# Warm-up operand made before the masks, first k issued by ScalarE, dilated q and k in 72 rows, and a new table of durations

## Chip, cores and metric

The kernel runs on one core of a Trainium2 chip. The metric is the device time of one execution in microseconds (us). Runs of the kernel before: 850.34 us median of 3 (850.1 to 851.13).

## What is computed

Attention with 8 heads over 4 batches of 576 tokens, head size 64, then two pairs of dense layers on the 2304 resulting rows of 512 features. Heads 0 to 3 see a window of the last 32 tokens (plain), heads 4 to 7 every fourth of the last 128 tokens (dilated). All is float32.

```python
mask_plain = (rel >= 0) & (rel < window)                                  # window = 32
mask_dil = (rel >= 0) & (rel < window * dilation) & (rel % dilation == 0) # dilation = 4
scores = np.where(masks[None, :, :, :], scores, -1000000000.0)
attn = np.exp(scores - np.max(scores, axis=-1, keepdims=True))
attn = attn / (np.sum(attn, axis=-1, keepdims=True) + 1e-09)
x = np.matmul(attn, v)            # -> (2304, 512)
h = x @ w_in;  x = (h - np.tanh(h)) @ w_out                               # first layer pair, d_ff 2048
h = x @ w_in2; out = (h * (1.0 / (1.0 + np.exp(-h)))) @ w_out2            # second layer pair
```

## The kernel before

A matrix product in the dense layers is made of three passes in a shorter float type (`passes`): each operand is split into a leading part and the rest. The weights of the first layer pair therefore go through a chain before TensorE may use them (class `Chunk`): a load on SP's queue (`load`), two steps on ScalarE (`prelu`, L203, and `lows`, L208), one on VectorE (`shift`, L213), one on GpSimd (`join`, L217), the leading part on ScalarE (`leading`, L169) and the rest on VectorE or GpSimd (`trailing`, L226).

The tokens are cut into five blocks, the first of 512 columns. While the first block goes through the first layer pair (16 slices f of d_ff, each with 12 matmuls `h<-x,w` and 12 `y<-gg,w`), the attention of the second batch is computed beside it. Ahead of that stands the attention of the first batch: four pairs of heads, c = 0 and 1 plain, c = 2 and 3 dilated. For each pair q, k and v are loaded; TensorE transposes q and k (`transpose_pe`) into a PSUM bank, half a tensor at a time; ScalarE or VectorE moves the half into qT or kT (`transposed`, through the helper at L169 to L173); then come scores (`products`, L458 and L467), maxima, exponentials (L516 or L525), sums, `normed` (L537), a transposition (L560), the product with v (`halves`, L576) and the split of the result into X (`x_hi` on ScalarE at L169, `x_lo` on VectorE at L631).

The pairs' q and k come in as rows of consecutive tokens (`load_in`): a plain pair as 96 rows of six tokens, a dilated pair as 128 rows of four tokens and a second piece of 16 rows. A plain tensor takes 2 loads (one for each head) and 6 transpositions of 96 rows; a dilated tensor 4 loads and 8 transpositions (128 and 16 rows for each of four classes).

The order of this whole stretch, up to the end of the first block, is set by a planner that runs when the program is built (`play`): every step is an `Op` with the engines that can take it and a cost on each, a rank, and for loads a landing time; the planner places the steps one by one on in-order engines. So a change of its costs moves steps on every engine. Where it expects TensorE to wait it puts in small matmuls on the constant `one` (`idle`, L109). Loads that SP and ScalarE issue share eight completion semaphores in turn; an issue waits for the load that had its semaphore before.

Ahead of the planned part stands a prologue in program order: the constants, `build_near()` (masks on GpSimd with three copies on VectorE, L270 to L278), then `warm`, set on VectorE (L1055), twelve matmuls on it (L1059), and one exponential on ScalarE over `warm` itself (L1060), which loads ScalarE's table.

```python
        build_near()
        warm = cpool.tile([P, 512], BF16, name="warm")
        nc.vector.memset(warm, 1.0)
        ...
        for n in range(WARM):
            nc.tensor.matmul(bank, warm[:, 0:P], warm, start=True, stop=True)
        nc.scalar.activation(out=warm[:, 0:1], in_=warm[:, 0:1], func=AF.Exp)
```

Of the kernel before, what the change touches and what calls it, by code (L numbers as in the profile page):

```python
# [8 lines left out]
F32 = mybir.dt.float32  # L9
# [10 lines left out]
P = 128  # L20
QB = 64
ROWS_P = 96
# [13 lines left out]
def tile_kernel(  # L36
# [251 lines left out]
    class Pair:  # L288
# [20 lines left out]
        def load_in(self, which, src):  # L309
            b, h0 = self.b, 2 * self.c  # L310
            if self.first:
                if self.dil:
                    t = wpool.tile([P, 2, DIL, 2, D], F32, tag="win", name=which)
                    parts = [(t[:, 0], src[b, h0:h0 + 2, :DIL * P]), (t[:CLS - P, 1], src[b, h0:h0 + 2, DIL * P:])]
                else:
                    t = wpool.tile([ROWS_P, S // ROWS_P, 2, D], F32, tag="win", name=which)
                    parts = [(t, src[b, h0:h0 + 2])]
                return t, [lambda e, j=j, out=out, x=x: e.dma_start(out=out[:, :, j], in_=x[j].rearrange("(p i) d -> p i d", i=out.shape[1]))  # L318
                           for out, x in parts for j in range(2)]
# [94 lines left out]
        def transpose_pe(self, which, half):  # L414

            dst = (self.qT, self.kT)[which]
            src = (self.qin, self.kin)[which]
            bank = ps_h.tile([P, 512], F32, tag="h", name="h")
            n = S // 2
            if self.dil:  # L420
                rest = CLS - P
                for m in range(2):
                    r, a = 2 * half + m, CLS * m
                    nc.tensor.transpose(bank[:, a:a + P], src[:, 0, r].rearrange("p j d -> p (j d)"), one[F32])
                    nc.tensor.transpose(bank[:, a + P:a + CLS], src[:rest, 1, r].rearrange("p j d -> p (j d)"), one[F32][:rest, :rest])
                self.moved = dst[:, n * half:n * (half + 1)], bank[:, :n]
            else:
                k = S // ROWS_P // 2
                for m in range(k):
                    i = k * half + m  # L430
                    nc.tensor.transpose(bank[:, ROWS_P * m:ROWS_P * (m + 1)], src[:, i].rearrange("p j d -> p (j d)"), one[F32][:ROWS_P, :ROWS_P])
                self.moved = (dst.rearrange("p (r i) -> p i r", i=2 * k)[:, k * half:k * (half + 1)],
                              bank[:, :n].rearrange("p (i r) -> p i r", i=k))
            return self.moved
# [554 lines left out]
    LANES, LAG_P, LAG_V = 8, 3.0, 2.0  # L989
# [35 lines left out]
    with tc.manual_schedule():  # L1025
# [27 lines left out]
        build_near()  # L1053
# [6 lines left out]
        nc.scalar.activation(out=warm[:, 0:1], in_=warm[:, 0:1], func=AF.Exp)  # L1060
# [8 lines left out]
        turned.append(opool.tile([P, NV, 2, 2, 32], F32, tag="wout", name="turned"))  # L1069
        in_room, out_room, stages = {}, {}, [(st1, NF * 2)]  # L1070
        for p in first:
            for w in range(2):
                got[p, w] = [op(QK_ON[p.c], fn, rank=p.c + 0.1 * w, late=0.6 if not p.dil or n < 2 else 0.1) for n, fn in enumerate(p.pieces(w))]
# [18 lines left out]
        for i, (p, (n0, n1)) in enumerate(units):  # L1092
            g, m = (n0, n1), n1 - n0
            r = p.rank + UNIT * n0 / NB
            if n0 == 0:
                moves = []
                for which in range(2):
                    for half in range(2):
# [3 lines left out]
                        moves.append(op({"V": 0.5, "A": 0.58} if p.dil else {"V": 0.38, "A": 0.31}, lambda e, p=p, w=which, held=held: p.transposed(e, w, held["m"]),  # L1102
# [28 lines left out]
            for z in range(2):  # L1131
                b = op({"A": 0.22 if p.dil else 0.33}, lambda e, p=p, n0=n0, z=z: p.x_hi(e, (n0, z)), [a], r)
                ends.append(op({"V": 0.23 if p.dil else 0.31}, lambda e, p=p, n0=n0, z=z: p.x_lo((n0, z)), [b], r))
# [19 lines left out]
        for n, ch in enumerate(chunks(0, w_in1, w_out1)):  # L1153
# [7 lines left out]
            b = op({"A": 0.57}, lambda e, ch=ch: ch.prelu(e), [a], due)  # L1161
            c = op({"A": 0.58}, lambda e, ch=ch: ch.lows(e), [a], due, port=True)
# [3 lines left out]
            b = op({"A": 0.56}, lambda e, ch=ch: ch.leading(e), [c, last_lead[ch.is_in], *room.get(f, ())], due, port=True)  # L1166
            last_lead[ch.is_in] = b
            c = op({"V": 0.75, "P": 1.3}, lambda e, ch=ch: ch.trailing(e), [b], due, port=True)
# [19 lines left out]
        def front(p):  # L1188
# [5 lines left out]
            a = op({"V": 1.09}, lambda e, p=p: p.transpose(0), [q_in, *left["q"]], r)  # L1194
            b = op({"V": 1.09}, lambda e, p=p: p.transpose(1), [k_in, *left["k"]], r)
# [3 lines left out]
            for n0, n1 in GROUPS:  # L1199
                m = (n1 - n0) / NB  # L1200
                d = op({"V": 0.1 + 0.7 * m}, lambda e, p=p, g=(n0, n1): p.masks(*g), [c], r + 2 + 4 * n0 / NB)
                left["bank"] += (d,)
                d = op({"V": 0.1 + 0.7 * m}, lambda e, p=p, g=(n0, n1): p.maxima(*g), [d], r + 2 + 4 * n0 / NB)
                exps.append(op({"A": 3.8 * m}, lambda e, p=p, g=(n0, n1): p.exps(*g), [d], r + 4 + 4 * n0 / NB))
# [8 lines left out]
        def back(p):  # L1213
            r = NEXT0 + NEXT * p.c
            v_in = v_of(p)
            ts = [op({"V": 0.4}, lambda e, p=p, j=j, n=n: p.p_quarter(j, n), [normed[p], *left["pT"]], r + 11 + 0.5 * n)
# [490 lines left out]
```

## Time and profile before

| what | us |
|---|---|
| median of 3 runs | 850.34 |
| the profiled execution | 849.79 |
| its span, first to last instruction | 848.0 |
| TensorE busy in the span | 829.5 |
| VectorE busy | 570.2 |
| ScalarE busy | 415.3 |
| GpSimd busy | 194.0 |

The profiled execution is 0.55 us below the median, and 1.8 us of it lie outside the span. Matmuls overlap in the records, so TensorE's busy time is not a measure of how well it is used; where it waits is read from its gaps. In the rows PE is TensorE, PEld its weight loads, DVE VectorE, ACT ScalarE, POOL GpSimd; SPq and ACTq are DMA issues on SP's and ScalarE's queues. In the page's slices of 21.2 us, PEclk is 8 tenths in the first two and 9 (90% or more) in all others.

### The profile page before, as it was taken

To read this page: it belongs to the slowest core of one execution; us is meant where nothing else is said; L and a number is where in the kernel's file an instruction comes from. 1 tells how busy PE (TensorE), PEld (TensorE's weight loads), DVE (VectorE), ACT (ScalarE), POOL (GpSimd) and SP (SyncE) were. 2 spreads that over 40 slices of the span, in tenths; PEclk is the share of its full clock that TensorE was granted. 3 is DMA by queue.
4 is the path that set the end of the run, shared out by engine and by line. 5 is a ranking of instruction groups with operands and counts; after the bars stand their busy time and mean duration, and the time that the engine had idled before them with its cause. 6 is when DMAs were issued, how large, how long until landed. Compare 5 with 4: busy or idle time off the path is not lost.

```text
span 848.0 us, 16638 instructions
## 1 busy us (share of the span) xinstructions
PE 829.5 (98%) x6226; PEld 735.7 (87%) x6226; DVE 570.2 (67%) x1008; ACT 415.3 (49%) x922; POOL 194.0 (23%) x232
## 2 busy tenths in 40 slices
PE   5899999999999999999999999999999999999998
PEld 3678887888887888888889999988899999999998
DVE  2568999457667655566664677547766897567764
ACT  2589876445456444566652343445323454223442
POOL 4654434033442331111100000010024200054000
PEclk8899999999999999999999999999999999999999
DMA  5599553636668423477759199839898676998541
GB/s 113 156 276 287 113 157 88 189 67 158 139 138 219 121 65 96 165 273 272 273 224 377 56 357 346 317 116 358 299 408 295 218 288 253 327 375 285 191 168 57
DMA packets 175487, 184.07 MB, mean 217 GB/s; under 512 B 98224, under 2 KB 138208, under 8 KB 174384
## 3 DMA queue, kind: packets, MB, share of 16 engines
q1 hardware_dynamic: 172784, 182.13, 66.3%
q8 instruction: 49, 0.80, 0.4%
q10 hardware_dynamic: 2368, 0.59, 0.3%
q0 software_dynamic: 256, 0.30, 0.2%
q14 instruction: 30, 0.25, 0.1%
HBM read 137.36 MB, written 45.61 MB: 216 GB/s over the span
## 4 chain that ended last, share of the span: by engine, by line
PE 83%; ACT 4%; DMA 4%; SPq 3%; issue 2%; DVE 2%; POOL 1%; POOLq 0%; DVEq 0%
PE y L656 40%; PE h L656 24%; PE q L656 16%; SPq L318 1%; DMA st<-in_moe_w_in_dram 1%; ACT prob L516 1%; DMA st<-in_moe_w_out_dram 1%; PE h L592 1%; DMA v<-in_v_dram 1%; ACT w L169 1%; DVE pT L550 1%; PE s L467 1%; PE y L1059 1%; ACT st L208 1%; SPq L324 1%
## 5 line engine op out<-in xcount | busy, mean ns | idle before, releaser
L656 PE MATMUL h<-x,w 128*128 128x512 f32 (+1 forms) x960 | 219.1, 370 | 1.3 <-DVE w L226 0.8
L656 PE MATMUL y<-gg,w 128*128 128x512 f32 (+1 forms) x960 | 218.0, 369 | 0.0
L656 PEld LDWEIGHTS h<-x,w 128*128 128x128 f32 x960 | 167.1, 189 | 33.2 <-DVE w L226 1.2
L656 PEld LDWEIGHTS y<-gg,w 128*128 128x128 f32 x960 | 167.4, 189 | 30.9 <-DVE gg L1248 0.7
L656 PE MATMUL y<-wr,gs 128*128 128x256 f32 (+1 forms) x840 | 123.5, 298 | 0.0
L656 PEld LDWEIGHTS y<-wr,gs 128*128 128x128 f32 x840 | 112.6, 191 | 4.6
L827 DVE TENSOR_TENSOR gs<-G,gs 128x768 fp32r<-128x768 f32 x64 | 62.7, 985 | 42.3 <-ACT gs L826 42.1
L804 ACT ACTIVATE G<-tmp 128x384 f32<-128x384 f32 (+1 forms) x48 | 32.9, 686 | 117.1 <-DVE tmp L795 117.1
L826 ACT ACTIVATE gs<-G 128x768 fp32r<-128x768 f32 x64 | 53.5, 844 | 70.1 <-PE y L656 44.1
L656 PE MATMUL q<-x,wr 128*128 128x384 f32 x432 | 82.8, 335 | 0.0
L683 DVE TENSOR_TENSOR g<-h,g 128x512 f32<-128x512 f32 (+1 forms) x64 | 39.8, 621 | 58.1 <-ACT g L682 57.7
L656 PEld LDWEIGHTS q<-x,wr 128*128 128x128 f32 x432 | 75.5, 188 | 0.5 <-DVE tmp L795 0.3
L1563 ACT ACTIVATE gg<-g 128x512 fp32r<-128x512 f32 (+1 forms) x64 | 37.1, 579 | 75.6 <-DVE g L683 73.4
L1565 DVE TENSOR_TENSOR gg<-g,gg 128x512 fp32r<-128x512 f32 (+1 forms) x64 | 40.1, 626 | 42.7 <-ACT gg L1563 40.6
L682 ACT ACTIVATE g<-h 128x512 f32<-128x512 f32 (+1 forms) x64 | 34.7, 542 | 67.7 <-PE h L656 66.0
L805 DVE SCALAR_TENSOR_TENSOR G<-G,tmp 128x384 f32<-128x384 f32 (+1 forms) x48 | 41.4, 862 | 34.3 <-ACT G L804 34.3
L217 POOL TENSOR_TENSOR st<-st 128x512 int32<-128x512 int32 x36 | 39.9, 1118 | 95.0 <-DVE st L213 54.4
L656 PE MATMUL y<-x,wr 128*128 128x384 f32 x288 | 57.8, 334 | 0.0
L656 PE MATMUL h<-x,wr 128*128 128x384 f32 x288 | 57.7, 334 | 0.0
L656 PE MATMUL q<-wr,gs 128*128 128x256 f32 (+1 forms) x348 | 57.6, 301 | 0.0
L656 PEld LDWEIGHTS q<-wr,gs 128*128 128x128 f32 x348 | 49.3, 191 | 2.3
L656 PEld LDWEIGHTS y<-x,wr 128*128 128x128 f32 x288 | 50.6, 188 | 0.2 <-DVE x L716 0.2
(177 smaller groups left out, 1141.0 us busy)
## 6 DMA issues: line engine op xcount, KB each, us to landing
wr<-w_in SPq DMA_DIRECT2D x72, 512.0 KB, 8.5
wr<-w_out SPq DMA_DIRECT2D x66, 512.0 KB, 5.3
st<-in_moe_w_in_dram SPq DMA_DIRECT2D x32, 256.0 KB, 5.6
st<-in_moe_w_out_dram SPq DMA_DIRECT2D x16, 512.0 KB, 5.9
st_in<-in_moe_w_in_dram SPq DMA_DIRECT2D x32, 256.0 KB, 4.5
w_in<-mixed SPq DMA_DIRECT2D x8, 1024.0 KB, 6.2
wr<-w_in SPq DMA_DIRECT2D x24, 256.0 KB, 8.5
x<-y_hi SPq DMA_DIRECT2D x6, 768.0 KB, 9.7
```

The source lines that it names most:

```text
L169: engine.activation(out=out, in_=in_, func=AF.Copy, scale=1.0 if scale is None else scale)
L208: engine.activation(out=low.bitcast(I32), in_=low, func=AF.Copy, scale=2.0 ** -29)
L217: engine.tensor_tensor(out=high, in0=high, in1=self.low.bitcast(I32), op=ALU.add)
L656: nc.tensor.matmul(o, stat[a], mov[b], start=first and n == 0, stop=last and n == 2, skip_group_check=more)
L682: nc.scalar.activation(out=g, in_=h, func=AF.Tanh)
L683: nc.vector.tensor_tensor(out=g, in0=h, in1=g, op=ALU.subtract)
L804: nc.scalar.activation(out=g, in_=h, func=AF.Tanh, scale=0.5)
L805: return lambda: nc.vector.scalar_tensor_tensor(out=g, in0=g, scalar=1.0, in1=h, op0=ALU.add, op1=ALU.mult)
L826: nc.scalar.activation(out=gs[:, 0], in_=g, func=AF.Copy)
L827: nc.vector.tensor_tensor(out=gs[:, 1], in0=g, in1=gs[:, 0].bitcast(F32), op=ALU.subtract)
L1563: nc.scalar.activation(out=gg[:, 0], in_=g, func=AF.Copy)
L1565: nc.vector.tensor_tensor(out=gg[:, 1], in0=g, in1=gg[:, 0].bitcast(F32), op=ALU.subtract)
```

## The change

Five things are edited.

1. `warm` is set before `build_near()`, and its matmuls are issued there. The exponential that loads ScalarE's table now reads `warm` and writes a tile of its own, `table`, and is a planned step.
2. The first pair's k is issued by ScalarE, the second pair's q and k by SP (before: the reverse).
3. Dilated q and k of the first batch come as 72 rows of eight tokens: 2 loads and 8 transpositions of 72 rows each. The move out of PSUM writes every second element (before: a contiguous half).
4. The seventh of the eight units of the first batch (pair 3, first group) takes its exponentials block by block with the maximum as bias, as the others with a 0 in `WHOLE`.
5. Costs and lags of the planner have other values, so that the order changes on all engines. Some of these lines stand below.

```diff
-                if self.dil:
-                    t = wpool.tile([P, 2, DIL, 2, D], F32, tag="win", name=which)
-                    parts = [(t[:, 0], src[b, h0:h0 + 2, :DIL * P]), (t[:CLS - P, 1], src[b, h0:h0 + 2, DIL * P:])]
-                else:
-                    t = wpool.tile([ROWS_P, S // ROWS_P, 2, D], F32, tag="win", name=which)
-                    parts = [(t, src[b, h0:h0 + 2])]
...
+                rows = ROWS_D if self.dil else ROWS_P
+                t = wpool.tile([rows, S // rows, 2, D], F32, tag="win", name=which)
+                return t, [lambda e, j=j: e.dma_start(out=t[:, :, j], in_=src[b, h0 + j].rearrange("(p i) d -> p i d", p=rows)) for j in range(2)]
...
+            rows = ROWS_D if self.dil else ROWS_P
+            k = S // rows // 2
+            for m in range(k):
+                nc.tensor.transpose(bank[:, rows * m:rows * (m + 1)], src[:, k * half + m].rearrange("p j d -> p (j d)"), one[F32][:rows, :rows])
+            dst = dst.rearrange("p (i c h) -> p h i c", i=k, h=2)[:, half] if self.dil else dst.rearrange("p (r i) -> p i r", i=2 * k)[:, k * half:k * (half + 1)]
+            self.moved = dst, bank[:, :S // 2].rearrange("p (i r) -> p i r", i=k)
...
-    QK_ON = {"S": 0.5}, {"S": 0.5, "A": 0.55}, {"S": 0.5}, {"S": 0.5}
-    V_ON = {"S": 0.55}, {"S": 0.55}, {"P": 0.65}, {"S": 0.55}
-    WHOLE = (1, 1, 1, 0, 1, 0, 1, 0)
+    SP, ACT = {"S": 0.66}, {"A": 0.68}
+    QK_ON = (SP, ACT), (SP, SP), (SP, SP), (SP, SP)
+    V_ON = {"S": 0.62}, {"S": 0.62}, {"P": 0.64}, {"S": 0.64}
+    WHOLE = (1, 1, 1, 0, 1, 0, 0, 0)
...
-        build_near()
         warm = cpool.tile([P, 512], BF16, name="warm")
         nc.vector.memset(warm, 1.0)
...
-        nc.scalar.activation(out=warm[:, 0:1], in_=warm[:, 0:1], func=AF.Exp)
+        build_near()
...
+        table = cpool.tile([P, 1], F32, name="table")
+        op({"A": 1.5}, lambda e: e.activation(out=table, in_=warm[:, 0:1], func=AF.Exp), rank=0.15)
...
-            b = op({"A": 0.57}, lambda e, ch=ch: ch.prelu(e), [a], due)
+            b = op({"A": 0.56}, lambda e, ch=ch: ch.prelu(e), [a], due, lag=LAG_W)
...
-        FREE = {"V": 5.3, "P": 4.8, "A": 0.9, "T": 6.3, "S": 0.5}
+        FREE = {"V": 5.2, "P": 4.9, "A": 0.75, "T": 6.3, "S": 0.5}
```

The order moves at three places of which the prediction speaks. The first is the start of SP's queue of DMA issues. Before (qin and kin are the raw tensors of a pair, v its values; the loads of pair 0, then v of pairs 0 and 1, then pair 2):

```order
L318 DMA qin<-in_q_dram 96x6x64 x2
L318 DMA kin<-in_k_dram 96x6x64 x2
L377 DMA v<-in_v_dram 128x4x64 x2
L378 DMA v<-in_v_dram 64x2x64
L377 DMA v<-in_v_dram 128x4x64 x2
L378 DMA v<-in_v_dram 64x2x64
L318 DMA qin<-in_q_dram 128x4x64 x2
L318 DMA qin<-in_q_dram 16x4x64 x2
L318 DMA kin<-in_k_dram 128x4x64 x2
L318 DMA kin<-in_k_dram 16x4x64 x2
```

Now, on the same queue, up to the first weights (st_204 is the stage of w_in for f = 0):

```order
L314 DMA qin<-in_q_dram 96x6x64 x2
L372 DMA v<-in_v_dram 128x4x64 x2
L373 DMA v<-in_v_dram 64x2x64
L314 DMA qin<-in_q_dram 96x6x64 x2
L314 DMA kin<-in_k_dram 96x6x64 x2
L372 DMA v<-in_v_dram 128x4x64 x2
L373 DMA v<-in_v_dram 64x2x64
L314 DMA qin<-in_q_dram 72x8x64 x2
L314 DMA kin<-in_k_dram 72x8x64 x2
L314 DMA qin<-in_q_dram 72x8x64 x2
L314 DMA kin<-in_k_dram 72x8x64 x2
L187 DMA st_204<-in_moe_w_in_dram 128x2x256 x2
```

Pair 0's k has left this queue and pair 1's q and k stand on it; a dilated tensor is one row of two loads. Before, 26 loads stand on SP ahead of st_204, now 20. Behind st_204 come, before, the load of st_205 and then the eight of pair 3's v; now six of pair 3's v and then st_205.

The second place is the start of ScalarE's program. Before:

```order
L1060 ACT_TABLE_LOAD
L1060 ACTIVATE warm<-warm 128x1
L318 DMA qin<-in_q_dram 96x6x64 x2
L318 DMA kin<-in_k_dram 96x6x64 x2
L169 ACTIVATE qT<-h 128x3x96 x2
L169 ACTIVATE kT<-h 128x3x96 x2
L169 ACTIVATE qT<-h 128x3x96
```

Now:

```order
L314 DMA kin<-in_k_dram 96x6x64 x2
L1057 ACT_TABLE_LOAD
L1057 ACTIVATE table<-warm 128x1
L169 ACTIVATE qT<-h 128x3x96
L169 ACTIVATE kT<-h 128x3x96
L169 ACTIVATE qT<-h 128x3x96
```

The loads stand ahead of the table load, and of the first pair's two halves ScalarE moves one; VectorE has the other.

The third place is ScalarE around the first weights (st_204 and st_205 are the stages of w_in for f = 0 and 1, x the split results of pair 1, prob the exponentials of pair 2). Before:

```order
L203 ACTIVATE st_204<-st_204 128x512
L169 ACTIVATE x<-s 128x2x16x4
L169 ACTIVATE x<-o 128x2x16x4
L208 ACTIVATE st_204<-st_204 128x512
L203 ACTIVATE st_205<-st_205 128x512
L208 ACTIVATE st_205<-st_205 128x512
L169 ACTIVATE x<-s 128x3x16x4
L169 ACTIVATE x<-o 128x2x16x4
L525 ACTIVATE prob<-prob 128x256
```

Now:

```order
L208 ACTIVATE st_204<-st_204 128x512
L203 ACTIVATE st_204<-st_204 128x512
L169 ACTIVATE x<-s 128x2x16x4
L169 ACTIVATE x<-o 128x2x16x4
L169 ACTIVATE x<-s 128x3x16x4
L169 ACTIVATE x<-o 128x2x16x4
L208 ACTIVATE st_205<-st_205 128x512
L169 ACTIVATE w<-st_204 128x512
L511 ACTIVATE prob<-prob 128x256
```

All of pair 1's results now stand ahead of the first step on st_205, and the leading part of st_204 right behind it. On TensorE the first three matmuls on weights (f = 0, c = 0) stand ahead of pair 3's scores; before, they stood behind them. Ahead of the first `y<-gg,w` 27 matmuls `h<-x,w` stand in one run, before 21.

## Rows read from the trace of the kernel before

**Rows 1.** The page, part 1: busy time, share of the span, instructions.
```profile
PE 829.5 (98%) x6226; PEld 735.7 (87%) x6226; DVE 570.2 (67%) x1008; ACT 415.3 (49%) x922; POOL 194.0 (23%) x232
```

**Rows 2.** Busy time by stretch: PE, PEld, DVE, ACT, POOL, granted clock, DMA share, GB/s.
```profile
15.00:21.50 6.50, 6.50 (x99) 5.33 (x100) 2.00 (x6) 3.30 (x6) 1.32 (x2) 0.50 0.63 143
...
34.70:45.50 10.80, 10.73 (x142) 7.32 (x142) 5.28 (x18) 6.29 (x21) 5.33 (x6) 0.53 0.75 234
45.50:53.10 7.60, 7.28 (x202) 5.67 (x201) 6.40 (x18) 7.08 (x25) 4.36 (x8) 1.00 1.05 382
36.20:55.60 19.40, 19.08 (x313) 13.84 (x313) 12.81 (x37) 15.44 (x50) 11.98 (x16) 0.76 0.94 302
53.10:140.00 86.90, 85.57 (x730) 68.17 (x727) 77.71 (x151) 74.26 (x193) 40.49 (x40) 1.00 0.67 165
```

**Rows 3.** Timeline, first 18 us: start, length, instruction, idle before and who ended it.
```profile
0.83 0.09 DVE L283 MEMSET kT<- 128x32 f32 x1 [0.83 <-PEq L1692]
...
5.61 0.48 DVE L1055 MEMSET warm<- 128x512 bf16 x1 [0.15 <-issue]
...
6.15 5.29 PE L1059 MATMUL y<-warm 128*128 128x512 bf16 x12 [6.15 <-DVE warm L1055]
...
11.47 0.21 ACT L1060 ACTIVATE warm<-warm 128x1 bf16<-128x1 bf16 x1 [4.01 <-PE y L1059]
11.48 1.37 ACTq L318 DMA_DIRECT2D qin<-in_q_dram  x2
...
14.26 1.19 ACT L169 ACTIVATE qT<-h 128x288 f32<-128x288 f32 x2 [2.58 <-issue]
...
14.99 0.74 PE L431 MATMUL h<-late,kin 96*128 96x96 f32 x3 [2.76 <-ACT qT L169]
...
17.14 0.42 PE L458 MATMUL y<-near,one 128*128 128x256 bf16 x1
```

**Rows 4.** Timeline of SP's queue: start and length of DMA issues.
```profile
3.55 1.18 SPq L377 DMA_DIRECT2D v<-in_v_dram  x2
14.44 0.66 SPq L378 DMA_DIRECT2D v<-in_v_dram  x1
...
17.01 2.60 SPq L318 DMA_DIRECT2D qin<-in_q_dram  x4
...
29.32 2.12 SPq L187 DMA_DIRECT2D st<-in_moe_w_in_dram  x4
31.48 5.32 SPq L372 DMA_DIRECT2D v<-in_v_dram  x8
```

**Rows 5.** The chain that ended last: start, length, what; just ahead of 14.44.
```profile
11.48 2.94 DMA qin<-in_q_dram
```

**Rows 6.** Timeline of TensorE, 21.7 to 60 us.
```profile
21.76 0.48 PE L431 MATMUL h<-late,kin 96*128 96x96 f32 x3
22.07 0.61 PE L109 MATMUL y<-one 128*128 128x128 bf16 x8
...
26.22 0.33 PE L424 MATMUL h<-late,qin 128*128 128x128 f32 x1
...
26.64 0.33 PE L424 MATMUL h<-late,qin 128*128 128x128 f32 x1
...
34.77 0.25 PE L576 MATMUL s<-turned,v 64*64 64x32 f32 x2 [2.72 <-DVE x L631]
...
59.35 0.97 PE L656 MATMUL y<-gg,w 128*128 128x512 f32 x3
```

**Rows 7.** Timeline of ScalarE: a dilated move, the first weights, the first tanh.
```profile
29.48 0.41 ACT L169 ACTIVATE kT<-h 128x288 f32<-128x288 f32 x1
33.38 0.65 ACT L203 ACTIVATE st<-st 128x512 f32<-128x512 f32 x1 [3.49 <-DMA st<-in_moe_w_in_dram]
...
36.22 0.67 ACT L203 ACTIVATE st<-st 128x512 f32<-128x512 f32 x1 [1.24 <-DMA st<-in_moe_w_in_dram]
...
55.61 0.60 ACT L1245 ACTIVATE g<-h 128x512 f32<-128x512 f32 x1
```

More of the change, by code (lines that the diff above doesn't have):

```diff
@@ L21 @@
 QB = 64
-ROWS_P = 96
+ROWS_P, ROWS_D = 96, 72
 KB = 96
@@ L418, in transpose_pe @@
             bank = ps_h.tile([P, 512], F32, tag="h", name="h")
[L419 to L433, printed above, removed]
+            rows = ROWS_D if self.dil else ROWS_P
[4 more added lines that the diff above has]
+            self.moved = dst, bank[:, :S // 2].rearrange("p (i r) -> p i r", i=k)
             return self.moved
@@ L1072, in tile_kernel @@
             for w in range(2):
-                got[p, w] = [op(QK_ON[p.c], fn, rank=p.c + 0.1 * w, late=0.6 if not p.dil or n < 2 else 0.1) for n, fn in enumerate(p.pieces(w))]
+                got[p, w] = [op(QK_ON[p.c][w], fn, rank=p.c + 0.1 * w, late=0.75 if p.dil else 0.65) for n, fn in enumerate(p.pieces(w))]
             v_in = [op(V_ON[p.c], fn, rank=p.c + 0.2, late=0.2 if p.dil else 0.5) for fn in p.v_loads()]
@@ L1101, in tile_kernel @@
                                [*got[p, which], *ring_h.take()], r - 2 + which * 0.1, ins=8 if p.dil else 6)
-                        moves.append(op({"V": 0.5, "A": 0.58} if p.dil else {"V": 0.38, "A": 0.31}, lambda e, p=p, w=which, held=held: p.transposed(e, w, held["m"]),
+                        moves.append(op({"V": 0.52, "A": 0.59}, lambda e, p=p, w=which, held=held: p.transposed(e, w, held["m"]),
                                         [a], r - 2 + which * 0.1))
@@ L1131, in tile_kernel @@
             for z in range(2):
-                b = op({"A": 0.22 if p.dil else 0.33}, lambda e, p=p, n0=n0, z=z: p.x_hi(e, (n0, z)), [a], r)
-                ends.append(op({"V": 0.23 if p.dil else 0.31}, lambda e, p=p, n0=n0, z=z: p.x_lo((n0, z)), [b], r))
+                b = op({"A": 0.18 if p.dil else 0.25}, lambda e, p=p, n0=n0, z=z: p.x_hi(e, (n0, z)), [a], r)
+                ends.append(op({"V": 0.22 if p.dil else 0.3}, lambda e, p=p, n0=n0, z=z: p.x_lo((n0, z)), [b], r))
             rings_o[n0].leave(*ends)
@@ L1193, in front @@
                 return
-            a = op({"V": 1.09}, lambda e, p=p: p.transpose(0), [q_in, *left["q"]], r)
-            b = op({"V": 1.09}, lambda e, p=p: p.transpose(1), [k_in, *left["k"]], r)
+            a = op({"V": 1.05 if p.dil else 0.73}, lambda e, p=p: p.transpose(0), [q_in, *left["q"]], r, lag=LAG_W)
+            b = op({"V": 1.07 if p.dil else 0.73}, lambda e, p=p: p.transpose(1), [k_in, *left["k"]], r, lag=LAG_W)
             c = op({"T": 1.7}, lambda e, p=p: p.plain_scores(), [a, b, *left["bank"], *ring_p.take()], r + 2, ins=16 * NB)
@@ L1264, in tile_kernel @@
             steps = g_steps(f)
-            a = op({"A": 0.52}, steps[1], [*hs, *(gate[-1:] if f else ())], r)
-            b = op({"V": 0.64}, steps[2], [a], r)
+            a = op({"A": 0.48}, steps[1], [*hs, *(gate[-1:] if f else ())], r)
+            b = op({"V": 0.61}, steps[2], [a], r)
             ring_h.leave(a, b)
@@ L1269, in tile_kernel @@
             c = op({"A": 0.55}, lambda e, f=f, s=steps: (put(f), s[3](e)), [b, *room], r, port=True)
-            d = op({"V": 0.65, "P": 1.35}, steps[4], [c], r, port=True)
+            d = op({"V": 0.61, "P": 1.3}, steps[4], [c], r, port=True)
             gate.append(d)
```

26 lines of the change are left out of this document (12 added, 14 removed).

## The prediction

> **What bounds the kernel now.** I read the page first: TensorE is busy for 829.5 of 848.0 us [rows 1]. Most of the program is therefore a queue of matmuls, and whatever another engine does matters only where TensorE waits or runs slowly. The second view, busy time by stretch, says where that is [rows 2]. From 53.1 to 140 us TensorE is busy for 85.57 of 86.9 us at a granted clock of 1.00 (2.4 GHz, the higher of the two levels). From 15 to 21.5 us the granted clock is 0.50 (1.2 GHz) and from 34.7 to 45.5 us 0.53. So the loss is in the first 53 us, the attention of the first batch. From the end of the attention at 53.1 us, and more strictly from the first `y<-gg,w` at 59.35 us [rows 6], the rest follows in one piece: if these points come x us earlier, the end comes x us earlier, as long as the other engines come x earlier too. That proviso is serious, since from 53.1 to 140 us VectorE is busy for 77.71 and ScalarE for 74.26 of 86.9 us [rows 2].
>
> The third view is the timeline of the first 18 us [rows 3], and it shows one chain of delays. VectorE sets `warm` only at 5.61 us, behind the mask copies, so TensorE's warm-up begins at 6.15 us and takes 5.29. ScalarE's exponential writes into `warm`, so it waits for the last matmul that reads it, 4.01 us, until 11.47. Only then does ScalarE issue pair 1's loads (1.37 us for the two of q, as much for k), and only then, at 14.26, does it move the first transposed q, for which TensorE waits 2.76 us. The fourth view shows what this does to a queue that seems to have no part in it: SP issues at 3.55 for 1.18 us and then nothing until 14.44 [rows 4], 9.7 us. In the chain of work, ScalarE's load of q stands just ahead of SP's next issue: it begins at 11.48 and takes 2.94 [rows 5], so SP waited for the completion semaphore that this late load held. Everything behind is late by this, up to the first weights, issued at 29.32. ScalarE gets them at 33.38 after waiting 3.49 us, and the next at 36.22 [rows 7]. Behind the first of these waits stands the split of pair 1's results, and so TensorE waits 2.72 us, until 34.77 [rows 6].
>
> **The change, part by part.** *Warm-up first.* `warm` now follows a memset that ends at 0.83 + 0.09 = 0.92; it takes 0.48, and the matmuls follow 0.06 later, as from 5.61 + 0.48 to 6.15 [rows 3]. They start at 1.46 instead of 6.15: 4.7 us earlier. The mask copies move behind it by 0.5 us at most; their result is first read by the scores at 17.14, so this costs nothing, and would cost 0.5 if the scores came at once.
>
> *ScalarE no longer waits.* It issues two loads of k (1.4 us) and its table load before anything is transposed. TensorE waited 2.76 us for the first move; what is left of that is at most the move itself, about 0.6, so 2.2 to 2.76 us go beyond the 4.7, and I take 2.5. The two halves of q, 1.19 us on ScalarE [rows 3], and those of k are shared with VectorE: about 0.6 us for the pair of them. The first scores come at 17.14 - 4.7 - 2.5 - 0.6 = 9.3 us, 7.8 earlier. Between 17.14 and 21.5 the clock was at its lower level [rows 2]; at the upper one these 4.4 us of matmuls take half if nothing else holds them. Between 0 and 2.2 us I take 1.0, since moves and maxima stand between them.
>
> *72 rows.* For 128 + 16 rows a class takes 26.64 - 26.22 = 0.42 us, four classes of a tensor 1.68. Three transpositions of 96 rows take 22.07 - 21.76 = 0.31, so 0.10 each [rows 6], and eight of 72 rows 0.83. The saving is 0.85 us a tensor at the upper clock, 1.7 for pair 2; the bounds are 0 (a price per instruction, 1.68 / 8 = 0.21) and 0.85, and I take 0.85 because 72 rows are nearest to the row with 96. The move now writes every second element: 0.41 us contiguous [rows 7], about 0.6 for a plain half with a stride of six (1.19 for two, [rows 3]). ScalarE makes three such moves; 0 to 0.6 us in all, of no weight beside the rest.
>
> Together TensorE would be at the point ahead of its 2.72 us wait, before at 34.77 - 2.72 = 32.0, at 32.0 - 7.8 - 1.0 - 1.7 = 21.5.
>
> *SP's queue.* The first weights were issued at 29.32. The 9.7 us of silence go. The sixteen loads of the dilated pairs took 29.32 - 17.01 = 12.3 us [rows 4], and eight of them go; by the shortest of these rows (2.60 for four) that is 5.2 us, by their mean 6.1. I take 5.2. Pair 1's four loads come onto the queue (2.7 us) and pair 0's two of k leave (1.3): 1.4 more. So 29.32 - 9.7 - 5.2 + 1.4 = 15.8, and they arrive 33.38 - 29.32 = 4.1 us later, at 19.9, 13.5 earlier. TensorE's step behind them comes at 21.5: the 2.72 us wait goes, with 1.6 us to spare. The second weights are now behind six loads of v (6 x 5.32 / 8 = 4.0 us [rows 4]): 15.8 + 1.1 + 4.0 = 20.9 to the issue, and with the same 4.1 they arrive at 25.0, 11.2 us earlier; with the 5.8 that the second took before (36.22 - 30.4) at 26.7, 9.5 earlier.
>
> A page of the Trainium skill speaks against the 72 rows: by "DMA: Bandwidth & Descriptors", section "Why a DMA increments its semaphore by 16 and not by 1", a load runs on the largest number of DMA engines up to 16 that divides its outer dimension, which makes 16 of 96 or 128 rows but only 12 of 72. No row here has 72, so no row bears on it yet. By that rule the data part of eight loads would be a third longer; a rough estimate from this page's count is 1 us more until the second weights, and the sum would be 13.2 instead of the 14.2 below; the rival of the second weights, further down, would then be the likelier one.
>
> *The clock.* With the 2.72 us wait gone, the cause of the slow stretch after it goes as well. At the upper level the 10.8 us at 0.53 would take some 5.4 less; 5.0 is what I take, between 0 and 5.4.
>
> **The sum.** TensorE alone: 7.8 + 1.0 + 1.7 + 2.7 + 5.0 = 18.2 us. But ScalarE must have carried the weights so far. Between the second weights (36.2) and the first tanh (55.6) it was busy for 15.44 of 19.4 us [rows 2]; by the order it has as many steps to do up to there as before, within one, so its busy time stays. It starts this stretch at 25.0 instead of 36.2. If it keeps all its idle time, 4.0 us, the tanh of 55.61 [rows 7] comes 11.2 earlier; if none, 15.2. Most of that idle time lay in the stretch of the slow clock, where it waited for TensorE, so I take three quarters as won: 14.2. The later end decides, so TensorE's 18.2 is cut to 14.2; TensorE will wait somewhat for the first weights and for the first `y<-gg,w`, and the run of 27 instead of 21 matmuls ahead of the latter hides part of it. The block exponentials of the seventh unit add some ScalarE time and take two steps from VectorE; they are in the same stretch and I count them as even. From there on the order differs in detail, but the same steps stand on the same engines, and I count nothing.
>
> 849.79 - 14.2 = 835.6 us for the profiled execution; it lies 0.55 below the median, so I predict 836.0 for the median. The likeliest case by itself spans 834 to 838.
>
> **The rivals.** *The weights keep up.* If ScalarE has next to no idle time and the second weights arrive a little sooner, all 18.2 us are won: 832.1. For it speaks that the silence of SP was the cause of nearly all lateness; against it, the loads of v that now stand ahead of the second weights. Chance 0.17.
>
> *The wait moves to the second weights.* ScalarE's step on st_205 stands ahead of the leading part of st_204, and the first three weight matmuls now stand ahead of pair 3's scores. If the second weights come at 26.7, TensorE stands idle for as long as it did before 14.99 and 34.77 (2.76 and 2.72 us), and the granted clock was 0.50 and 0.53 after both [rows 2, 3, 6]. Then the 5.0 us of the clock are not won, and the sum is 14.2 - 5.0 = 9.2: 841. For it: the clock fell after both waits of that length; against it: by the 4.1 us of the first weights TensorE would wait less. Chance 0.19.
>
> *The gain is taken back.* From 53.1 to 140 us VectorE and ScalarE have under 13 us of slack each [rows 2]. If the new order puts weight steps behind attention steps there, TensorE waits for weights; 5 us more than now makes 841. Against it: TensorE's gaps in that stretch are 1.3 us in all. Chance 0.14.
>
> *Nothing is won*, because the silence of SP returns at another load: about 850. Only two loads are left on ScalarE, and nothing stands ahead of them. Chance 0.02.
>
> *Slower.* If loads arrive too late for the early warm-up, TensorE idles between them and the clock stays at 0.50 all through the attention. Before, 15.2 of the 36 us after 17.14 were at the lower clock (4.4 + 10.8), 2.7 waiting and the remaining 18.1 at the upper one. All at the lower: 15.2 + 36.2 = 51.4 us from 9.3 on, 60.7 instead of 53.1 us, less some 3.4 for the shorter transpositions: 4 us slower, 854. It decides itself at waits of about 2.7 us that come again within each ten; before there were two. Chance 0.03.
>
> **How the numbers follow.** The forecast has 0.45, the others 0.17, 0.19, 0.14, 0.02 and 0.03. About 0.2% (1.7 us) is what a measurement can tell from no change. Faster by more: 0.45 + 0.17 + 0.19 + 0.14 = 0.95; within: 0.02; slower: 0.03. The range reaches from 831 (all 18.2 us and one of the later gaps) to 843 (either of the two lesser gains, with 2 us for the bounds of the clock and of the landing).
>
> **What would show it.** Right: the warm-up begins near 1.5 us; ScalarE's first move lies before 8; SP has no gap over 2 us before the first weights, which are issued near 16 us; the first tanh lies near 41.4. Wrong: a granted clock of 0.50 for over 7 us between 9 and 40, a wait of ScalarE for the second weights beyond 27 us, or gaps of TensorE of over 4 us between 45 and 140.

## The result and the profile after

| | before | after |
|---|---|---|
| median, us | 850.34 (5 runs, 847.01 to 851.69) | 837.12 (5 runs, 835.72 to 840.49) |
| ratio | 1 | 0.9856 [0.9825, 0.9888] |
| profiled execution, us | 849.79 | 837.03 |
| its span, us | 848.0 | 835.3 |

The change makes the kernel 1.4% faster. The forecast was 836.0 and the range 831 to 843. Run again beside later experiments, the changed kernel took 840.58 (837.48 to 842.76; ratio 0.9879 [0.9861, 0.9898]), and the ten executions have a median of 839.0. The middle half of them lies between 837.1 and 840.8; of the 61 executions of before it lies between 850.1 and 851.6, with single ones up to 858.0. That scatter matters below.

The page of after, part 1, answers to [rows 1]:

```profile
PE 823.1 (99%) x6231; PEld 732.5 (88%) x6231; DVE 568.3 (68%) x1006; ACT 413.5 (50%) x926; POOL 200.3 (24%) x235
```

Busy time hardly moved on any engine. What went is time in which TensorE stood or ran slowly at the start. Its timeline in the first 10 us, against [rows 3]:

```profile
1.52 4.43 PE L1045 MATMUL y<-warm 128*128 128x512 bf16 x12 [1.52 <-DVE warm L1041]
...
9.33 0.44 PE L417 MATMUL h<-late,qin 96*128 96x96 f32 x3 [0.61 <-ACT kT L169]
...
9.67 0.27 PE L444 MATMUL y<-near,one 128*128 128x256 bf16 x1
```

The warm-up starts at 1.52 instead of 6.15, the wait of 2.76 us for the first move is one of 0.61, and the first scores come at 9.67 instead of 17.14 (forecast 9.3). SP's queue, from pair 1's k on, against [rows 4]:

```profile
5.72 1.31 SPq L314 DMA_DIRECT2D kin<-in_k_dram  x2
...
9.16 1.76 SPq L314 DMA_DIRECT2D qin<-in_q_dram  x2
10.97 2.19 SPq L314 DMA_DIRECT2D kin<-in_k_dram  x2
13.20 1.87 SPq L314 DMA_DIRECT2D qin<-in_q_dram  x2
15.11 1.63 SPq L314 DMA_DIRECT2D kin<-in_k_dram  x2
16.79 1.37 SPq L187 DMA_DIRECT2D st<-in_moe_w_in_dram  x2
18.20 2.91 SPq L367 DMA_DIRECT2D v<-in_v_dram  x6
21.15 0.94 SPq L187 DMA_DIRECT2D st<-in_moe_w_in_dram  x2
```

The silence of 9.7 us is gone; each issue follows the one before. The first weights are issued at 16.79 (before 29.32, forecast 15.8). The eight loads of 72 rows take from 9.16 to 16.79, 7.6 us; the sum had left 12.3 - 5.2 = 7.1 for them. Two of them take 1.63 at the least, two of 96 rows 1.31 in the first line. ScalarE, against [rows 7]:

```profile
21.70 0.68 ACT L208 ACTIVATE st<-st 128x512 int32<-128x512 uint32 x1 [1.12 <-DMA st<-in_moe_w_in_dram]
...
26.78 0.69 ACT L208 ACTIVATE st<-st 128x512 int32<-128x512 uint32 x1 [1.19 <-DMA st<-in_moe_w_in_dram]
27.36 0.66 ACT L169 ACTIVATE w<-st 128x512 fp32r<-128x512 f32 x1
...
43.97 0.64 ACT L1233 ACTIVATE g<-h 128x512 f32<-128x512 f32 x1
```

The first weights reach ScalarE 11.7 us earlier than before, the first tanh 11.6 earlier (forecast 41.4, so 2.6 late). TensorE, against [rows 6]:

```profile
16.79 0.67 PE L417 MATMUL h<-late,qin 72*128 72x72 f32 x8
18.39 0.25 PE L562 MATMUL s<-turned,v 64*64 64x32 f32 x2 [0.93 <-DVE turned L171]
...
20.70 0.52 PE L546 MATMUL y<-late,prob 128*128 128x128 f32 x3 [0.80 <-ACT kT L169]
...
29.85 1.63 PE L642 MATMUL h<-x,w 128*128 128x512 f32 x3
...
41.27 7.13 PE L642 MATMUL h<-x,w 128*128 128x512 f32 x27
48.24 1.98 PE L642 MATMUL y<-gg,w 128*128 128x512 f32 x8
```

Eight transpositions of 72 rows take 0.67 us where four classes took 1.68: 1.0 us a tensor, a little more than the 0.85 of the forecast. The waits are 0.93 and 0.80 us where one of 2.72 stood. Last, busy time by stretch, against [rows 2] (columns as there):

```profile
14.70:21.50 6.80, 5.07 (x155) 4.23 (x155) 6.14 (x17) 4.45 (x19) 6.06 (x9) 1.00 0.92 215
22.00:32.20 10.20, 9.97 (x167) 7.69 (x170) 6.42 (x18) 7.71 (x24) 5.20 (x7) 0.50 0.85 277
32.20:45.40 13.20, 11.74 (x235) 8.24 (x227) 9.73 (x26) 10.75 (x39) 7.08 (x10) 1.00 1.07 310
...
53.10:140.00 86.90, 86.88 (x766) 70.48 (x765) 73.88 (x150) 70.06 (x186) 41.71 (x44) 1.00 0.59 155
```

One of the two stretches at the lower clock is gone, the other is not: it lies at 22.0 to 32.2 us, with TensorE busy for 9.97 of the 10.2 us; eight transpositions of 72 rows take 1.22 us there (at 26.84), where they took 0.67 at 16.79. From 53.1 to 140 us TensorE is busy for all but 0.02 us; nothing is taken back there.

### The profile page after: what moved, and what is told of

It reads as the page before. It is cut to its first block, busy times and chain, and to the rows that moved or that the text cites. A ratio compares the mean times of both kernels' runs of the same rounds, so it can differ in the third digit from the quotient of the medians.

```text
span 835.3 us, 16623 instructions
## 1 busy us (share of the span) xinstructions
PE 823.1 (99%) x6231; PEld 732.5 (88%) x6231; DVE 568.3 (68%) x1006; ACT 413.5 (50%) x926; POOL 200.3 (24%) x235
## 4 chain that ended last, share of the span: by engine, by line
PE 89%; DVE 3%; ACT 3%; DMA 2%; issue 1%; POOL 0%; SPq 0%; DVEq 0%; POOLq 0%; ACTq 0%
PE y L642 42%; PE h L642 26%; PE q L642 16%; PE s L453 1%; DVE pT L536 1%; DMA w_out<-o_mixed 1%; ACT prob L502 1%; PE h L578 1%; PE y L453 1%; DMA qin<-in_q_dram 1%; PE o L453 1%; PE s L562 1%; DVE g L669 0%; ACT gg L1551 0%; PE s L578 0%
```

## The experiments

My theory was the prediction's: the first 53 us are governed by when the weights come, and that by SP's queue. Its rivals were that the order of the steps carries the gain, that the 72 rows win nothing, and that the lower clock is what costs. Twelve runs, all with a median of 4 to 12 executions beside runs of the kernel before, whose median was 850.5 to 850.8 each time. A thirteenth, with 48 rows of twelve tokens in place of 72 of eight (e12), needed more on-chip memory than was left and has no time, so the form of the 72 rows is not tested by itself. The runs are listed by when SP issued the first weights; this and the starts of the first and the 17th tanh on ScalarE are from the one profiled execution, the median is of all:

| kernel | first weights, us | first tanh, us | 17th tanh, us | median, us | ratio to before |
|---|---|---|---|---|---|
| before | 29.32 | 55.61 | 150.66 | 850.5 | 1 |
| before + numbers (e6) | 28.76 | 55.82 | 153.35 | 849.55 | 0.9981 [0.9961, 1.0] |
| before + early warm-up (e1) | 24.69 | 52.93 | 148.47 | 846.13 | 0.9947 [0.9929, 0.9964] |
| before + own table tile (e2) | 23.67 | 50.11 | 147.95 | 846.83 | 0.9961 [0.9946, 0.9977] |
| after, swap undone (e10) | 22.28 | 47.32 | 140.08 | 842.78 | 0.9889 [0.9861, 0.9917] |
| after, old numbers (e5) | 22.06 | 46.90 | 146.15 | 845.0 | 0.994 [0.9924, 0.9957] |
| after, 128 + 16 rows (e4) | 21.64 | 45.53 | 143.01 | 845.32 | 0.9936 [0.992, 0.9952] |
| before + early warm-up + own tile (e3) | 21.55 | 49.90 | 146.01 | 844.58 | 0.9927 [0.9907, 0.9947] |
| after, four waits filled (e11) | 17.81 | 44.23 | 138.29 | 837.5 | 0.9833 [0.9807, 0.9858] |
| after again | 17.59 | 45.52 | 139.58 | 840.58 | 0.9879 [0.9861, 0.9898] |
| after, lead first (e8) | 17.16 | 45.90 | 142.27 | 841.62 | 0.9888 [0.9861, 0.9914] |
| after, more filled (e13) | 16.85 | 43.31 | 137.11 | 837.75 | 0.9843 [0.9806, 0.9881] |
| after | 16.79 | 43.97 | 137.59 | 837.12 | 0.9856 [0.9825, 0.9888] |
| after, two waits filled (e7) | 16.51 | 45.83 | 140.02 | 839.65 | 0.9865 [0.985, 0.9879] |

In the main the medians go with the first weights. Every kernel with them at 21 to 23 us takes 842.8 to 845.3, whatever it has of the change otherwise, and every one with them below 18 takes 837 to 842. That is an ordering of whole kernels, in which other things move too, and the two groups nearly touch. The tanh columns say more. The 17th tanh is the first of the second block, and from there to the end all fourteen kernels need 697.3 to 698.3 us: the whole difference between them is made in the first block. Up to the first tanh only a part of it is made. From the first to the 17th it is 95.1 us before and 93.6 in the changed kernel, but 92.8 in e10 and 99.3 in e5. The single runs follow.

**The prologue.** e1 moves `build_near()` of the kernel before behind the warm-up; e2 lets the exponential write its own tile; e3 does both.

```diff
-        build_near()
         warm = cpool.tile([P, 512], BF16, name="warm")
         nc.vector.memset(warm, 1.0)
...
+        build_near()
-        nc.scalar.activation(out=warm[:, 0:1], in_=warm[:, 0:1], func=AF.Exp)
+        table = cpool.tile([P, 1], F32, name="table")
+        nc.scalar.activation(out=table, in_=warm[:, 0:1], func=AF.Exp)
```

> The kernel before with one edit: warm is set ahead of the mask copies, and the warm-up matmuls and the exponential (which still writes into warm) follow it at once. Theory (one chain: warm-up, then ScalarE's wait for it, then ScalarE's loads, then SP's silence): warm-up starts at 1.5 instead of 6.15 us, ScalarE is free at about 6.5 instead of 11.47, SP's silence ends at about 9.7 instead of 14.4, the first weights are issued at about 24.6 instead of 29.3. TensorE and the weights move alike by 4.7 us, so the wait of 2.7 us and the slow clock after it stay: 845.5 us, 844 to 847. Rival (the gain of the changed kernel comes from the new durations and the order they make): under 1.5 us, 849 to 851.

> The kernel before with one edit: the exponential that loads ScalarE's table writes a tile of its own, so it no longer waits for the warm-up matmuls; warm is still set behind the mask copies. Theory: ScalarE issues its loads from about 7.7 instead of 11.48 us, SP's silence ends near 10.7 instead of 14.4, the first weights are issued 3.8 us earlier, near 25.5; the first move of q comes at about 11.8 instead of 14.26, since the warm-up itself has not moved. TensorE is then 2.4 us earlier and the weights 3.8, so the wait of 2.7 us shrinks to about 1.3: 846.5 us, 843 to 848, the lower part if the clock does not fall after the shorter wait. Rival (only the warm-up's own 4.7 us count, the queue behind is hidden): 849 to 851.

> The kernel before with both edits of the two runs above and nothing else: old loads, old durations, old order but for the prologue. Theory: warm-up from 1.5 us, ScalarE's loads from about 3, SP's silence nearly gone (it ends near 6), first weights issued near 21 instead of 29.3 (8.3 us earlier), TensorE 7.2 us earlier at the first scores: 841.5 us, 838 to 843; the lower part if the slow clock goes with the wait. So two thirds of the gain of the changed kernel, or more. Rival (order and durations carry it): 846 or more.

Measured: 846.13, 846.83 and 844.58; the first two are as expected. Each edit alone ends about half of SP's silence, and both together give less than the sum. SP's queue in e1, at the silence:

```profile
3.55 1.18 SPq L377 DMA_DIRECT2D v<-in_v_dram  x2
9.74 0.67 SPq L378 DMA_DIRECT2D v<-in_v_dram  x1
```

In the chain of work of e1, ScalarE's load of q just ahead of 9.74:

```profile
6.54 3.19 DMA qin<-in_q_dram
```

The same queue in e3, up to the first weights:

```profile
3.64 2.75 SPq L377 DMA_DIRECT2D v<-in_v_dram  x2
6.43 0.67 SPq L378 DMA_DIRECT2D v<-in_v_dram  x1
...
9.01 3.18 SPq L318 DMA_DIRECT2D qin<-in_q_dram  x4
...
21.55 2.13 SPq L187 DMA_DIRECT2D st<-in_moe_w_in_dram  x4
```

The silence ends at 9.74 in e1 (before at 14.44), again just as ScalarE's load of q has landed (6.54 + 3.19); in e3 all that is left of it is an issue of 2.75 us instead of 1.18, as the theory of the shared semaphore has it. Sixteen loads still stand behind it, from 9.01 to 21.55. But e3 gives 6 us, not the 9 expected, though the first weights were issued about where they were expected (21). What is missing lies behind their issue: they reach ScalarE at 26.82, 5.3 us later, TensorE waits 3.28 us for the split of pair 1's results, and its granted clock is 0.50 from 21 to 41 us.

**The numbers alone** (e6): the kernel before with the planner's new costs and `WHOLE`.

> The kernel before with the planner's new numbers alone (costs, lags, WHOLE, free times): prologue, loads and transpositions stay as before. Theory: the chain from the late warm-up to SP's silence is untouched, the first weights are issued near 29 us: 850 us, 847 to 853. Rival (the order carries the gain): 843 or less.

849.55: about 1 us by themselves, with an interval from 0 to 3.3.

**The 72 rows taken back** (e4): the changed kernel with the old `load_in` and transpositions, four loads a tensor.

```diff
-    rows = ROWS_D if self.dil else ROWS_P
+    if self.dil:
+        t = wpool.tile([P, 2, DIL, 2, D], F32, tag="win", name=which)
+        parts = [(t[:, 0], src[b, h0:h0 + 2, :DIL * P]), (t[:CLS - P, 1], src[b, h0:h0 + 2, DIL * P:])]
```

> The changed kernel with the dilated q and k of the first batch in their old form: 128 and 16 rows, four loads and eight transpositions of both sizes a tensor. Theory (the weights are held back by the loads ahead of them on SP's queue): sixteen loads at about 0.65 us take the place of eight that took 7.6 us together, so the first weights are issued near 21 instead of 16.8 us, and TensorE spends 0.85 us more on each dilated tensor: 841 (839 to 843). Rival (72 rows win nothing, since each of their loads took 0.95 us to issue instead of 0.65, and a queue that is short of engines lands later): 836 to 838, as the changed kernel.

845.32, more than expected. **The numbers taken back** (e5): costs, lags and `WHOLE` of the kernel before in the changed one.

> The changed kernel with the planner's costs, lags and choice of whole units of the kernel before; the early warm-up, the table load's own tile, the swap of k and q and the 72 rows stay. Theory (what wins is that the first weights come early, whatever the order behind them): they are still issued near 17 us and the run takes 840 (838 to 842). Rival (the order of the steps carries the half of the gain that the early start does not): 843 to 845.

845.0: the first weights were not issued near 17 us, so the condition of the theory was not met, and the time is the rival's. SP's queue in e4, up to the first weights:

```profile
9.33 2.60 SPq L318 DMA_DIRECT2D qin<-in_q_dram  x4
...
19.01 2.59 SPq L318 DMA_DIRECT2D kin<-in_k_dram  x4
21.64 2.81 SPq L187 DMA_DIRECT2D st<-in_moe_w_in_dram  x4
```

And in e5, from pair 3's k on:

```profile
15.93 1.63 SPq L314 DMA_DIRECT2D kin<-in_k_dram  x2
17.60 4.41 SPq L367 DMA_DIRECT2D v<-in_v_dram  x7
22.06 2.10 SPq L187 DMA_DIRECT2D st<-in_moe_w_in_dram  x4
```

Two different causes, one effect on the queue. In e4 sixteen loads stand ahead of the weights; in e5 the loads are eight, but the planner with its old costs puts seven loads of v (4.41 us) there. Either way the weights are issued at 22 us, and the median lies 4.4 to 4.7 us above that of the changed kernel beside them (840.58).

The late weights are not the whole of that. Against the profile of the changed kernel the first tanh comes 1.6 us later in e4 and 2.9 in e5, but the 17th 5.4 and 8.6 later. Most is lost between the two, where TensorE stands again. Its busy time from 60 to 140 us in e5, where the granted clock is 0.98 as well:

```profile
60.00:140.00 80.00, 75.62 (x613) 60.62 (x613) 65.39 (x132) 59.92 (x163) 38.79 (x38) 0.98 0.56 134
```

In e4 it is 78.23, in the changed kernel 79.98. So in these two orders a part of the gain is taken back, as one rival of the prediction had it; which step makes TensorE stand there was not looked into. The 72 rows and the numbers thus win together what neither wins alone: e4 has the numbers without the rows, e5 the rows without the numbers, and both stand where e3 stands with neither. In e5 TensorE also waits 2.57 us for a load of q and 3.09 for ScalarE's move of one, so it is not a test of the weights alone.

**The swap undone** (e10): `QK_ON = (SP, SP), (ACT, ACT), (SP, SP), (SP, SP)`.

> The changed kernel with the swap undone: the first pair's k on SP again, the second pair's q and k on ScalarE, which now waits for nothing before it issues them. SP then has two loads fewer, but the order puts seven loads of v ahead of the first weights. Theory (the place of these loads matters only through the first weights on SP's queue): first weights issued near 18.9 us (16.8 + 1.3 - 2.7 + 3.5), and 840 to 842. Rival (the swap carries part of the gain by itself, since the second pair's loads now hold semaphores that SP needs): a gap of SP of over 2 us ahead of 15 us, and 843 or more.

842.78. The weights were issued at 22.28, 3.4 us later than expected, and again 4.53 us of that are seven loads of v:

```profile
3.85 2.10 SPq L372 DMA_DIRECT2D v<-in_v_dram  x2
7.24 0.67 SPq L373 DMA_DIRECT2D v<-in_v_dram  x1
...
17.71 4.53 SPq L367 DMA_DIRECT2D v<-in_v_dram  x7
22.28 2.00 SPq L187 DMA_DIRECT2D st<-in_moe_w_in_dram  x4
```

SP stands still from 5.95 to 7.24, less than the rival's 2 us. But the ratio, 0.9889, lies within the interval of the changed kernel run again (0.9861 to 0.9898), and the profiled execution, with the weights at 22.28, is the fastest of its six (839.81). That the swap wins anything is not shown, and neither is that weights 5.5 us later cost here what they seem to cost in e4 and e5.

**The same program again.**

> The changed kernel once more, beside the next three. Both theories: 837 (836 to 839). What it shows besides is how far the stretch at the lower granted clock moves between two profiled executions of one program: in the first it was 21.98 to 32.22 us. If the waits of TensorE set it, it stands in the same place; if something outside the program does, it does not.

840.58, more than expected. The stretch at the lower clock began in the same place and lasted longer, as two of its stretches show:

```profile
22.00:32.20 10.20, 9.54 (x148) 7.26 (x150) 6.60 (x18) 6.43 (x21) 4.58 (x6) 0.51 0.70 202
32.20:41.30 9.10, 8.32 (x194) 6.23 (x193) 5.53 (x16) 7.35 (x30) 4.84 (x9) 0.80 1.04 365
```

Its waits of TensorE are the same 0.93 and 0.80 us; its second weights were issued at 23.01 instead of 21.15 and its first tanh came at 45.52. So most of what the two executions differ by (2.1 us) lies in these first 50 us.

**The lead first** (e8): ScalarE's two steps on st_205 made to follow the leading part of st_204.

```diff
-            c = op({"A": 0.56}, lambda e, ch=ch: ch.lows(e), [a], due, port=True)
+            c = op({"A": 0.56}, lambda e, ch=ch: ch.lows(e), [a, last_lead[True] if n == 1 else None], due, port=True)
```

> The changed kernel with ScalarE's steps on the second weights (st_205) made to follow the leading part of the first (st_204), which it has at hand. Theory (TensorE's first three matmuls on weights are held by ScalarE's wait of 1.19 us for the second weights): the leading part is ready before 26.5 instead of 28.0 us, the first h<-x,w starts 1 to 2 us earlier and the run takes 1 us less than the changed kernel, 836 to 838. Rival (at the lower clock TensorE gets to these matmuls only near 29.5 us, whatever the weights): first h<-x,w at 29 to 30 us, and no change, 837 to 840.

841.62, above the 837 to 840 of the rival too; the first `h<-x,w` is at 30.25. The theory falls. ScalarE's row says what held the leading part (the step on the first weights is at 21.98):

```profile
27.50 0.68 ACT L169 ACTIVATE w<-st 128x512 fp32r<-128x512 f32 x1 [1.15 <-POOL st L217]
```

Freed from the second weights, it waits for GpSimd's `join` of the first, to the same moment as in the changed kernel (27.36).

**Filling the waits.** e7 puts small matmuls on the constant into the two waits of 0.93 and 0.80 us; e11 fills three further places; e13 fills more. All the work of the kernel stays.

```diff
+            for m in range({(2, 0, 1): 14, (2, 1, 0): 12, (3, 0, 1): 8}.get((self.c, which, half), 0)):
+                nc.tensor.matmul(bank[:, 384:512], one[BF16], one[BF16], start=True, stop=True)
...
+            for m in range({0: 12}.get(n0, 18) if self.first and self.c == 3 else 0):
+                nc.tensor.matmul(bank[:, 384:512], one[BF16], one[BF16], start=True, stop=True)
```

(e7 has the first two entries of the first loop; e11 as shown; e13 has 24 in place of 8, and 12 behind pair 3's k.)

> The changed kernel with 26 small matmuls on the constant put into the two waits of TensorE of 0.93 and 0.80 us that stand ahead of 21.98 us; they only add work. Theory (the arrival of the weights sets when the first three matmuls on them can start, near 29.6 us, so that the lower clock ahead of that costs little): 836 (835 to 837.5). Rival (the stretch of 10.2 us at the lower clock is a loss of its own, and it was these two waits that brought it): the granted clock stays at 1.00 and the run takes 833 (832 to 834). A third result, the lower clock in another place or of another length with no change of the waits, says that waits of this size do not set it.

> The run that filled two waits of TensorE, with 38 more small matmuls: 8 behind the transposition of pair 3's q, 12 and 18 ahead of the last two transpositions of exponentials, where it then waited 0.71 and 1.14 us and the granted clock fell at 36.30 us. They only add work. Theory (waits of 0.7 to 1.2 us that come close together bring the lower clock): no stretch at 0.50 from 10 to 60 us and 834 (832.5 to 836). Rival (the lower clock comes in the attention whatever the waits): a stretch of 7 to 14 us at 0.50 somewhere between 20 and 50 us and 838 to 840.

> The run with all four fillings, with 16 more small matmuls behind pair 3's q and 12 behind its k, where TensorE then waited 1.23 and 1.02 us just ahead of the fall of the granted clock at 30.22 us. They only add work. Theory (such waits bring the lower clock): no stretch at 0.50 from 5 to 60 us, and 836 (834.5 to 837.5). Rival (the lower clock comes whatever the waits): a stretch at 0.50 of 3 us or more between 15 and 50 us, and 837 to 839.

Medians 839.65, 837.5 and 837.75, all above what the theories had (836, 834 and 836). In e7 the clock stays up through the place where it fell before, and falls later, behind two other waits. Busy time by stretch in e7:

```profile
22.00:32.20 10.20, 8.21 (x228) 6.22 (x231) 7.98 (x22) 7.45 (x24) 5.96 (x8) 1.00 0.87 271
...
36.30:46.50 10.20, 9.76 (x90) 7.49 (x91) 5.36 (x15) 6.31 (x15) 4.20 (x4) 0.50 0.96 258
```

TensorE's rows in e7 around that fall:

```profile
35.17 0.44 PE L548 MATMUL y<-late,prob 128*128 128x128 f32 x2 [0.71 <-POOL prob L525]
36.74 0.90 PE L548 MATMUL y<-late,prob 128*128 128x128 f32 x3 [1.14 <-POOL prob L525]
...
41.59 8.74 PE L644 MATMUL h<-x,w 128*128 128x512 f32 x27
```

The gain of the earlier place is given back in the run of 27 `h<-x,w`, 8.74 us instead of 7.13; there the first tanh waits 1.51 us for TensorE, so in e7 the lower clock does cost. e11 fills those too; two waits of another place grew there, and the clock was low for only some 3.4 us behind them. TensorE's rows in e11:

```profile
27.50 0.83 PE L417 MATMUL h<-late,kin 72*128 72x72 f32 x8 [1.23 <-DVE qT L173]
29.35 0.38 PE L109 MATMUL h<-one 128*128 128x128 bf16 x4 [1.02 <-DVE kT L171]
```

e13 fills these as well. Its busy time from 9.6 to 60 us, all of it at a granted clock of 1.00:

```profile
9.60:60.00 50.40, 47.46 (x913) 37.98 (x912) 39.57 (x94) 41.17 (x115) 31.70 (x39) 1.00 0.96 258
```

So the fillings move the stretch at the lower clock from place to place, and with all of them it does not come (the mean granted clock of e13's four executions is 0.999 to 1.000). That it is the wait that brings the lower clock does not follow: a filling closes a wait and adds matmuls of 128 columns as well, and in e3 the clock fell without a wait (last section). Yet without the slow stretch the median is 837.75, against 839.0 for the ten of the changed kernel (the cost of the fillings included), a difference of 1.3 us that is within the scatter, and not 5. The 17th tanh comes at 137.11 instead of 137.59. ScalarE's rows of e13 say why:

```profile
25.78 0.70 ACT L208 ACTIVATE st<-st 128x512 int32<-128x512 uint32 x1 [0.55 <-DMA st<-in_moe_w_in_dram]
...
43.31 0.57 ACT L1237 ACTIVATE g<-h 128x512 f32<-128x512 f32 x1
```

From the second weights to the first tanh it takes 17.5 us at the upper clock, against 43.97 - 26.78 = 17.2 in the changed kernel with the stretch at the lower one. In both ScalarE is busy for 14.74 us of that. The chain of the weights hides nearly all of the lower clock here. e11 has the lowest ratio of all runs, but its interval overlaps with that of the changed kernel; that it beats it is not shown.

## Why the prediction was right, and where its terms were off

*Right in place, and in what decides.* Warm-up 1.52 (forecast 1.46); first scores 9.67 (9.3); SP's silence gone and first weights issued at 16.79 (15.8); TensorE's 2.72 us wait gone. The cut was right in kind as well: not TensorE's own 18.2 us but the weights' chain on ScalarE decided. The first tanh of the changed kernel waits for nothing, and e13, where TensorE has no slow stretch, has it only 0.7 us earlier (43.31 instead of 43.97).

*Mis-sized: the weights' chain.* The forecast had the second weights at 25.0 and the tanh 16.4 us later, at 41.4. Measured: 26.78 and 17.2 later, at 43.97. So 14.2 was 11.6. Of the missing 2.6 us, 1.8 are the arrival: the issue at 21.15 was only 0.25 late, but the way to ScalarE took 5.6 us where 4.1 were counted (the prediction kept 5.8, and so 26.7, as its later end). The other 0.8 are ScalarE's: it was busy for 14.74 us instead of 15.44, but idle for 2.45 instead of 1.0. The idle time does not go with the slow clock, as the prediction took it to: in e13, without a slow stretch, it is 2.79.

The first weights were 1.0 us late, half of it from the eight loads of 72 rows, 7.6 us instead of 7.1. The rule of the Trainium skill that the prediction set against the 72 rows ("DMA: Bandwidth & Descriptors", section "Why a DMA increments its semaphore by 16 and not by 1") put the weights 1 us later and the sum at 13.2, nearer to what came. No run here shows the rule at work: what the rows show is dearer issues (0.79 us at the least for one, 0.60 for 96 rows), and the way that was longer is that of the weights, which have 128 rows. Even so e4, with all 128 + 16 rows, is slower by 4.7 us.

*Wrong: the clock.* "With the 2.72 us wait gone, the cause of the slow stretch after it goes as well" failed. With no wait above 0.93 us the clock was at 0.50 for 10.2 us, nearly as long as before. One of the prediction's own signs of being wrong, a granted clock of 0.50 for over 7 us between 9 and 40, thus came. The rival of the second weights had this fall of the clock, with the wrong cause: TensorE does not stand still for the second weights, and e8 shows no gain from their place in ScalarE's order. Its price was wrong too: by the prediction's own rule the 5.0 us come off TensorE's 18.2, not off the 14.2 to which that had been cut. That leaves 13.2 for TensorE, and with the second weights at 26.7 the chain gives 9.5 + 3.0 = 12.5 and decides again: this rival should have stood near 837.3, not at 841. That the wrong term cost the forecast so little is luck in part: the 5.0 us were among those that the chain took away anyway.

*Not counted: the rest.* From the first tanh to the end it is 848.0 - 55.61 = 792.4 us before and 835.3 - 43.97 = 791.3 after; TensorE's 1.3 us of gaps from 53.1 to 140 are gone, and the run of 27 hides the wait for the first `y<-gg,w`. These 1.1 us and the 11.6 make the 12.7 of the profiled execution. In the second profiled execution it was 10.1 and 0.5. The forecast counted nothing here; the rival that the gain is taken back fell for the changed kernel, while in e4 and e5 a part was taken back.

*Open.* Of the gain, the prologue alone gives 6 us (e3). The rest needs the 72 rows and the numbers together; how much of it is the place of the weights and how much the order behind them is not separated. The seventh unit's block exponentials were counted as even and not tried by themselves. Why the same program issued its second weights 1.9 us later in one execution than in another was not settled.

## What to carry to other kernels

Look for a load that is issued late on one queue and stalls another through a shared semaphore: its price is paid by everything behind it, here 9.7 us on SP for two loads of ScalarE. Test fewer loads and the order together, since here neither alone was worth much: with the loads gone and the old costs (e5), other loads moved up into their place. Compare kernels at a late point from which on all take equally long, here the 17th tanh, and not only at the first one that looks decisive. And before counting on a faster stretch of one engine, find the chain that ends next: here filling the waits kept the clock up, and of the 5 us expected from that the medians have 1.3, which is within the scatter.

## What the runs showed of the hardware that was not expected

In the changed kernel the granted clock fell to 0.50 (1.2 GHz) for 10.2 us behind two waits of TensorE of 0.93 and 0.80 us, in e7 behind 0.71 and 1.14 us, and for some 3.4 us in e11 behind 1.23 and 1.02; with the waits of a place filled it did not fall there. But a wait need not stand ahead of the fall. In e3 TensorE was busy, by its records, all through the six microseconds ahead of it, mostly with matmuls of 32 to 128 columns:

```profile
15.00:21.00 6.00, 6.00 (x134) 4.42 (x132) 4.82 (x15) 3.88 (x18) 5.41 (x10) 1.00 0.42 90
21.00:41.00 20.00, 16.72 (x270) 11.99 (x272) 8.00 (x23) 9.46 (x28) 9.38 (x12) 0.50 0.79 252
```

The wait of 3.28 us in e3 ends at 28.21, well after the fall. What the fillings did, whether they closed waits or added matmuls, is therefore open.

In the ten executions of the changed kernel the mean granted clock of the span lies between 0.986 (840.49 us) and 0.996 (835.72 us), and the longer ones are mostly those with the lower clock. But e11 and e13, at 0.997 to 1.000, take 835.89 to 840.04, so executions differ by 4 us without it too; how much of the ten's scatter is the price of the clock is not shown.

In the changed kernel a load of 72 rows took SP at least 0.79 us to issue, one of 96 rows at least 0.60, and a tensor's two loads of 72 rows up to 2.19.
